# Taking the paddings out ahead of the feed-forward tiles of a Fourier mixer: the same program at other SBUF addresses

## The chip, the core and the metric

The kernel runs on one core of one Trainium2 chip. The metric is the device time of one execution in microseconds; the kernel before stands at 2060.12 us, the median of three runs (2059.15 to 2062.64).

## What is computed

The reference, cut to what matters (4 sequences of 3072 tokens, width 256):

```python
X = np.fft.rfft(x, axis=1)                      # Fourier mixing
Yr = Xr @ w_r - Xi @ w_i + b_r;  Yi = Xr @ w_i + Xi @ w_r + b_i
Y = soft_threshold(Yr, 0.01) + 1j * soft_threshold(Yi, 0.01)
x = np.fft.irfft(Y, n=3072, axis=1)
xk = mu_k * x + (1 - mu_k) * x_prev;  xr = mu_r * x + (1 - mu_r) * x_prev
k = np.maximum(xk @ w_k, 0)                     # first feed-forward, 256 -> 1024 -> 256
x = 1 / (1 + np.exp(-(xr @ w_rr))) * ((k * k) @ w_v)
h = x @ w_in                                    # second feed-forward, 256 -> 2048 -> 256
return (h * np.clip(h + 3, 0, 6) / 6) @ w_out
```

## The kernel before

Every matrix is held as two float32r parts, a rounded high part (`_hi`, `h`) and the rest (`_lo`, `l`), and a product is three matmuls: high by high, low by high, high by low. In a row of the trace a matmul reads `out<-moving,weights` or with the two inputs in the other order; the instruction's first operand in the code is the stationary one (the weights of the array, 128 columns, loaded by a LDWEIGHTS of its own), the second is the moving one.

Three kinds of work follow each other. The Fourier stages (`s1`, `s2`, `mix`, `ia`, `ib`) are woven with the first feed-forward: for each of 24 token tiles of 512 there is one unit `pr` (12 matmuls), four of `pk` (12 each) and four of `acc` (12 each), so 2592 matmuls with 512 moving columns. In `pr` and `pk` the weights `wr`, `wk` are stationary and the inputs `kh`, `kl` move; in `acc` the weights `wv` are stationary and the squared outputs `gh`, `gl` move. The second feed-forward's first tile (`pi`, 512 columns) runs in between. From the second tile on, each of 184 units (23 tiles by 8) has 45 matmuls of 256 moving columns: 21 of a Strassen-like product (into `rq` and `cc`), whose stationary operand is either a sum of weights (`sw`) or a part of the weights (`wi`) and whose moving operand is an input or a sum of inputs (`xh`, `xl`, `th`, `tl`); and 24 into `oacc`, where the gate outputs `gh`, `gl` are stationary and `wo` moves. The code lists all instructions of each engine in a fixed order.

Tiles of one pool lie one behind the other in each partition of SBUF, and nearly every size is a multiple of 256 bytes. So a small tile that is never used, made by `pad(pool, n)`, shifts all that the pool (and the pools opened behind it) allocates later by n bytes modulo 256. Such calls stand ahead of several groups of tiles.

Of the kernel before, what the change touches and what calls it, by code (L numbers as in the profile page):

```python
# [103 lines left out]
def fourier_mix_ffn_kernel(  # L104
# [33 lines left out]
    kb = ctx.enter_context(tc.tile_pool(name="kb", bufs=1))  # L138
    kw = ctx.enter_context(ExitStack())
    kw_p = kw.enter_context(tc.tile_pool(name="kw", bufs=1))  # L140
# [3 lines left out]
    def pad(pool, n):  # L144

        pads.append(n)
        pool.tile([128, n // 4], F32, name=f"pad{len(pads)}")
# [82 lines left out]
                running.append(w.decode(w.load(stage, *job), *job))  # L230
            yield

    padded = []

    def stage1():
        w = kb.tile([128, 1024], U32, tag="gh", bufs=3, name="stw")
        t = kb.tile([128, 2, TOK], F32, tag="gl", bufs=3, name="stt")
        if not padded:
            padded.append(pad(kb, 128))
        return w, t  # L240

    with tc.manual_schedule(engines=order):
# [249 lines left out]
            later.append(plan("ib", b, 0, 8))  # L492

        aw = [Weights(fp, w, 2, D, f"aw{i}") for i, w in enumerate((w_r, w_i))]
        pad(kw_p, 64)
        wr = Weights(kw_p, w_rr, 2, D, "wr")
        wk = Weights(kw_p, w_k, 2, FF1, "wk")
        pad(kw_p, 128)
        wv = Weights(kw_p, w_v, 8, D, "wv")

        nc.gpsimd.dma_start(out=f1.rearrange("p s n -> p (s n)"), in_=small[:, 0 : 2 * N1])
# [117 lines left out]
        def load_2(i):  # L619
            b, t = tiles[i]  # L620
            v = sc_x[b].rearrange("a p n -> p a n")[:, :, TOK * t : TOK * t + TOK]
            a = kb.tile([128, 2, TOK], F32, tag="xf", bufs=1, name="xa2")
            nc.sync.dma_start(out=a, in_=v)
            xt[i] = a
# [7 lines left out]
        def u_i(i, j, between=()):  # L632

            xh, xl = xt[i]
            p = ptile("pi")
            for m in range(2):
                c = slice(256 * j + 128 * m, 256 * j + 128 * m + 128)
                three(
                    p[:, 512 * m : 512 * m + 512],
                    [((wi.hi[:, k, c], wi.lo[:, k, c]), (xh[:, k], xl[:, k])) for k in range(2)],  # L640
                )
            g = kb.tile([128, 1024], F32, tag="g", bufs=2, name="g2")
            h = kb.tile([128, 1024], F32R, tag="gh", bufs=3, name="gh2")
            l = kb.tile([128, 1024], F32R, tag="gl", bufs=3, name="gl2")
            nc.scalar.activation(g, p, AF.Relu, bias=half, scale=1.0 / 6.0)
            nc.vector.scalar_tensor_tensor(g, g, 1.0, p, op0=ALU.min, op1=ALU.mult)
            nc.scalar.activation(h, g, AF.Copy)
            for f in between:
                f()
            nc.vector.tensor_sub(l, g, h.bitcast(F32))  # L650
            hg[i, j] = (h, l)
# [7 lines left out]
        def sums(sp, c):  # L659

            j = slice(2 * c, 2 * c + 2)
            h, l = (w[:, :, j] for w in sw)
            tmp = {}

            def full():
                a = tmp["a"] = kb.tile([128, 4, 2, 128], F32, tag="yt", bufs=1, name="wa")
                for k in range(2):
                    for m in range(2):
                        hi, lo = (
                            w[:, k, 512 * c : 512 * c + 512]  # L670
                            .rearrange("p (j m f) -> p j m f", j=2, m=2)[:, :, m]
                            .bitcast(F32)
                            for w in (wi.hi, wi.lo)
                        )
                        nc.vector.tensor_add(a[:, 2 * m + k], hi, lo)

            def four():
                a11, a12, a21, a22 = (tmp["a"][:, n] for n in range(4))
                t = tmp["t"] = sp.tile([128, 4, 2, 128], F32, tag="t", bufs=1, name="ws")
                nc.vector.tensor_add(t[:, 0], a21, a22)  # L680
                nc.vector.tensor_sub(t[:, 1], t[:, 0], a11)
                nc.vector.tensor_sub(t[:, 2], a11, a21)
                nc.vector.tensor_sub(t[:, 3], a12, t[:, 1])

            return [
                (full, None),
                (four, lambda: nc.scalar.activation(h, tmp["t"], AF.Copy)),
                (lambda: nc.vector.tensor_sub(l, tmp["t"], h.bitcast(F32)), None),
            ]
# [215 lines left out]
        def decode_to(n):  # L905

            nonlocal done2
            while done2 < n:
                next(jobs2, None)
                done2 += 1  # L910
# [74 lines left out]
        for n, (i, j) in enumerate(units):  # L985
            if i == 0:
                decode_to(max(done2 + 2, 2 * (j // 2 * 2 + 1) + 7, 2 * (8 + j) + 7))
                if j == 3:
                    decode_to(len(wi.jobs + wo.jobs) * 2 + 5)
                    stage.close()  # L990
                    sp = ctx.enter_context(tc.tile_pool(name="sp", bufs=1))
                    pad(sp, 64)
                    sw = [sp.tile([128, 4, 8, 128], F32R, name=f"sw{c}") for c in range(2)]
                    pad(sp, 192)
                    c0, c1, c2, c3 = (sums(sp, c) for c in range(4))
                    x1 = split_s(sp, 1)

                    beside = {
                        3: ([x1[0][0]], [x1[0][1]]),
                        4: ([x1[1][0]], [x1[1][1], c0[0][0]]),  # L1000
                        5: ([x1[2][0]], [c0[1][0]]),
                        6: ([c1[0][0]], [c0[1][1], c0[2][0]]),
                        7: ([c1[1][0]], [c1[1][1]]),
                    }
                    both = lambda f, g: lambda: (f(), g())
                    aside = [(both(c1[2][0], c2[0][0]), None), c2[1], (both(c2[2][0], c3[0][0]), None)] + c3[1:]
                u_i(i, j, beside[j][0] if j >= 3 else ())
                if lag:
                    u_v(*lag.pop(0))
                    if not lag:  # L1010
                        kw.close()
                elif j > 2:
                    for f in u_o(*pend.pop(0)):
                        f()
                if j >= 3:
                    for f in beside[j][1]:
                        f()
            else:
                if (i, j) == (1, 0):
                    banks.close()  # L1020
                    pz = ctx.enter_context(tc.tile_pool(name="pz", bufs=6, space=PSUM))
                before = u_s(sp, pz, i, j, u_o(*pend.pop(0)), before, aside.pop(0) if aside else (None, None))
            pend.append((i, j))
            if i + 1 < len(tiles):
                if j == (1 if i else 0):
                    load_2(i + 1)
                if j == 3 and i:
                    aside += split_s(sp, i + 1)
# [28 lines left out]
```

## Time and profile before

| | |
|---|---|
| median of three runs | 2060.12 us |
| the profiled execution: its time / its span | 2060.34 / 2058.6 us |
| TensorE matmul busy | 2000.5 us, 97% of the span, 13928 matmuls |
| TensorE weight load busy | 1848.1 us, 90% |
| VectorE / ScalarE busy | 1529.6 us (74%) / 1353.3 us (66%) |
| mean granted TensorE clock | 0.982 of full |

How to read it: a matmul's busy time in the records includes the emptying of the array, so neighbours overlap. What a matmul costs in a full queue is the distance from its start to the next one's start. In the steady stretches below, recorded length minus distance is 163 ns throughout (281 against 118, 276 against 113), so that a group's mean length shows its distance as well.

### The profile page before, as it was taken

How to read it: one execution, taken by the hardware profiler on the slowest of the kernel's cores; microseconds unless marked ns; L12 is line 12 of the kernel's file. 1: busy time of each engine (PE TensorE's matmuls, PEld its weight loads, DVE VectorE, ACT ScalarE, POOL GpSimd, SP SyncE). 2: the span in 40 equal slices, each digit the busy share in tenths (PEclk: the TensorE clock that was granted, in tenths of full speed). 3: DMA queues.
4: the chain of work that ended last, by engine and by line, in shares of the span. 5: the costliest groups of instructions: out<-in, count | busy, mean ns of one | idle time of the engine just before them, and what ended most of it. 6: DMA issues, size and time to landing. Idle time of an engine off the chain costs nothing.

```text
span 2058.6 us, 33814 instructions
## 1 busy us (share of the span) xinstructions
PE 2000.5 (97%) x13928; PEld 1848.1 (90%) x13928; DVE 1529.6 (74%) x1929; ACT 1353.3 (66%) x1965; POOL 34.6 (2%) x63
## 2 busy tenths in 40 slices
PE   5889999999999999999999999999999999999999
PEld 3868888888788888877789999999999999999998
DVE  3778667766776687887878777777777777777775
ACT  5567557655765566666557766677666776677675
POOL 0000000000000000000000000000000000000000
PEclk7978999999999999999999999999999999999999
DMA  9775337543653352222101010010100110010100
GB/s 259 232 220 184 116 115 230 166 143 112 222 171 113 94 159 90 76 86 76 52 21 31 23 32 22 22 32 22 32 22 25 29 32 21 22 32 22 32 11 22
DMA packets 106989, 175.86 MB, mean 85 GB/s; under 512 B 12945, under 2 KB 63314, under 8 KB 106834
## 3 DMA queue, kind: packets, MB, share of 16 engines
q1 hardware_dynamic: 96034, 141.76, 22.4%
q0 software_dynamic: 10480, 31.67, 5.6%
q8 instruction: 109, 1.79, 0.4%
q14 instruction: 46, 0.38, 0.1%
q10 hardware_dynamic: 320, 0.26, 0.0%
HBM read 110.35 MB, written 63.31 MB: 84 GB/s over the span
## 4 chain that ended last, share of the span: by engine, by line
PE 80%; DVE 10%; ACT 5%; DMA 3%; issue 1%; SPq 0%; ACTq 0%; DVEq 0%
PE oacc L824 25%; PE rq L824 15%; PE acc L163 9%; PE pk L163 8%; PE cc L824 6%; PE mix L163 5%; PE s L163 4%; PE pr L163 2%; DVE g L591 2%; DVE gl L592 1%; PE ia L163 1%; PE ib L454 1%; PE pi L163 1%; PE ib L455 1%; DVE xf L549 1%
## 5 line engine op out<-in xcount | busy, mean ns | idle before, releaser
L824 PE MATMUL oacc<-wo_hi,gl 128*128 128x256 f32 x1536 | 431.6, 281 | 0.5 <-DVE gl L798 0.5
L824 PE MATMUL oacc<-wo_hi,gh 128*128 128x256 f32 x1536 | 430.7, 280 | 0.0
L824 PE MATMUL oacc<-wo_lo,gh 128*128 128x256 f32 x1536 | 430.4, 280 | 0.0
L824 PEld LDWEIGHTS oacc<-wo_hi,gh 128*128 128x128 f32 x1536 | 293.1, 191 | 0.2
L824 PEld LDWEIGHTS oacc<-wo_hi,gl 128*128 128x128 f32 x1536 | 289.3, 188 | 0.9 <-DVE gl L798 0.7
L824 PEld LDWEIGHTS oacc<-wo_lo,gh 128*128 128x128 f32 x1536 | 288.4, 188 | 0.0
L780 DVE TENSOR_TENSOR c<-rq,s 128x512 f32<-128x512 f32 x184 | 127.3, 692 | 182.9 <-ACT s L776 182.9
L793 DVE SCALAR_TENSOR_TENSOR g<-g,c 128x1024 f32<-128x1024 f32 x184 | 225.4, 1225 | 40.3 <-ACT g L792 35.0
L797 ACT ACTIVATE gh<-g 128x1024 fp32r<-128x1024 f32 x184 | 194.8, 1059 | 48.7 <-DVE g L793 48.6
L798 DVE TENSOR_TENSOR gl<-g,gh 128x1024 fp32r<-128x1024 f32 x184 | 223.7, 1216 | 1.2 <-ACT gh L797 1.2
L824 PE MATMUL rq<-th,sw 128*128 128x256 f32 x1104 | 222.1, 284 | 0.8 <-ACT s L771 0.6
L792 ACT ACTIVATE g<-c,half 128x1024 f32<-128x1024 f32 x184 | 210.7, 1145 | 4.3 <-DVE c L781 3.5
L760 ACT ACTIVATE s<-rq 128x512 f32<-128x512 f32 x184 | 110.3, 599 | 125.0 <-PE rq L824 123.1
L591 DVE TENSOR_TENSOR g<-g 128x1024 f32<-128x1024 f32 x96 | 117.4, 1222 | 79.8 <-ACT gh L590 79.8
L824 PEld LDWEIGHTS rq<-th,sw 128*128 128x128 f32 x1104 | 168.7, 188 | 1.6 <-ACT s L771 1.0
L163 PE MATMUL acc<-gl,wv_hi 128*128 128x512 f32 x384 | 153.4, 399 | 4.4 <-DVE gl L592 4.3
L824 PE MATMUL rq<-tl,sw 128*128 128x256 f32 x552 | 154.9, 281 | 0.0
L163 PE MATMUL pk<-kh,wk_hi 128*128 128x512 f32 x384 | 152.5, 397 | 0.8 <-ACT g L586 0.8
L163 PE MATMUL acc<-gh,wv_hi 128*128 128x512 f32 x384 | 153.2, 399 | 0.0
L163 PE MATMUL acc<-gh,wv_lo 128*128 128x512 f32 x384 | 152.6, 397 | 0.0
L163 PE MATMUL pk<-kh,wk_lo 128*128 128x512 f32 x384 | 151.6, 395 | 0.0
L163 PE MATMUL pk<-kl,wk_hi 128*128 128x512 f32 x384 | 151.4, 394 | 0.0
(152 smaller groups left out, 4902.4 us busy)
## 6 DMA issues: line engine op xcount, KB each, us to landing
tt<-in_tab_dram POOLq DMA_DIRECT2D x40, 640.0 KB, 4.8
yt<-sc_y SPq DMA_DIRECT2D x23, 608.0 KB, 4.0
a<-in_x_dram SPq DMA_DIRECT2D x64, 192.0 KB, 3.8
sc_a<-s1sb SPq DMA_DIRECT2D x32, 384.0 KB, 3.7
a<-sc_a SPq DMA_DIRECT2D x48, 256.0 KB, 3.2
sc_b<-iasb SPq DMA_DIRECT2D x48, 256.0 KB, 4.3
a<-sc_b SPq DMA_DIRECT2D x64, 192.0 KB, 3.1
sc_y<-ysb SPq DMA_DIRECT2D x32, 384.0 KB, 2.8
```

What stands on the lines that cost most here:

```text
L163: nc.tensor.matmul(o, a, c, start=first and i == 0, stop=last and i == n - 1, **kw)
L454: nc.tensor.matmul(o, h[:, i, e], r, start=True, stop=False)
L455: nc.tensor.matmul(o, l[:, i, e], r, start=False, stop=True)
L549: nc.vector.scalar_tensor_tensor(o, y[:, a, 0 : hi - lo], mus[:, w, a : a + 1], o, op0=ALU.mult, op1=ALU.add)
L591: nc.vector.tensor_mul(g, g, g)
L760: nc.scalar.activation(s[:, 1:3].rearrange("p a n -> p (a n)"), rq, AF.Copy)
L780: nc.vector.tensor_add(c[:, 1::2], two(rq), s[:, 0:2])
L792: nc.scalar.activation(g, c, AF.Relu, bias=half, scale=1.0 / 6.0)
L793: nc.vector.scalar_tensor_tensor(g, g, 1.0, c, op0=ALU.min, op1=ALU.mult)
L797: lambda: nc.scalar.activation(h, g, AF.Copy),
L798: lambda: nc.vector.tensor_sub(l, g, h.bitcast(F32)),
L824: return lambda: nc.tensor.matmul(o, lhs, rhs, start=start, stop=stop, skip_group_check=True)
```

## The change

Five `pad` calls go: one in the pool `kb` behind the tiles `gh`, `gl`; two in `kw_p`, ahead of `wr` and ahead of `wv`; two in `sp`, ahead of the weight sums and ahead of the tiles behind them. No instruction, no order and no wait changes on any engine; line numbers behind the edits drop by 4 to 8. Only start addresses move:

| tiles | address modulo 256 before | after |
|---|---|---|
| `kh`, `kl`, `xh`, `xl`, `xf`, `g`, `r`, `yt` (pool `kb`) | 160 | 32 |
| `th`, `tl`, `s`, `c`, temporaries (pool `sp`) | 160 | 32 |
| `wr`, `wk` | 224 | 32 |
| `wv` | 96 | 32 |
| `sw` | 224 | 32 |
| `gh`, `gl` | 32 | 32 |
| `wi`, `wo` | 224 | 224 |
| all tiles of the Fourier stages | | unchanged |

```diff
-    padded = []
-
     def stage1():
         w = kb.tile([128, 1024], U32, tag="gh", bufs=3, name="stw")
         t = kb.tile([128, 2, TOK], F32, tag="gl", bufs=3, name="stt")
-        if not padded:
-            padded.append(pad(kb, 128))
         return w, t
...
         aw = [Weights(fp, w, 2, D, f"aw{i}") for i, w in enumerate((w_r, w_i))]
-        pad(kw_p, 64)
         wr = Weights(kw_p, w_rr, 2, D, "wr")
         wk = Weights(kw_p, w_k, 2, FF1, "wk")
-        pad(kw_p, 128)
         wv = Weights(kw_p, w_v, 8, D, "wv")
...
                     sp = ctx.enter_context(tc.tile_pool(name="sp", bufs=1))
-                    pad(sp, 64)
                     sw = [sp.tile([128, 4, 8, 128], F32R, name=f"sw{c}") for c in range(2)]
-                    pad(sp, 192)
                     c0, c1, c2, c3 = (sums(sp, c) for c in range(4))
```

The text below speaks of a **pair**: a matmul's moving operand and the stationary operand of the matmul behind it, whose load runs beside it. A pair's **distance apart** is the stationary address minus the moving address, modulo 256. All slices begin at multiples of 256 bytes within their tiles here, so the table above gives it. Pairs in a unit of the second feed-forward, and in the first feed-forward:

| pairs | before | after |
|---|---|---|
| 24 pairs that `oacc` streams, per unit | 21 at 64, 3 at 0 (ahead of `rq`) | 24 at 64 |
| 21 pairs that `rq` and `cc` stream, per unit | 18 at 64, 3 at 128 (ahead of `oacc`) | 12 at 0, 9 at 192 |
| 2592 that `pr`, `pk`, `acc` stream | 2401 at 64, the rest at hand-overs | 2536 at 0 |
| 96 that `pi` streams | 89 at 64 | 89 at 192 |

## Rows read from the trace of the kernel before

**Rows 1.** The page: span, and busy time of each engine with instruction counts.
```profile
span 2058.6 us, 33814 instructions
...
PE 2000.5 (97%) x13928; PEld 1848.1 (90%) x13928; DVE 1529.6 (74%) x1929; ACT 1353.3 (66%) x1965; POOL 34.6 (2%) x63
```

**Rows 2.** Busy time by stretch: length, each engine, then PEclk, DMA share, GB/s.
```profile
400.00:820.00 420.00, 417.88 (x2414) 361.96 (x2413) 293.31 (x370) 260.46 (x364) 13.26 (x23) 1.00 0.44 136
820.00:1060.00 240.00, 235.62 (x1044) 189.69 (x1043) 196.10 (x239) 145.18 (x174) 0.00 (x0) 1.00 0.21 68
1075.00:1600.00 525.00, 524.69 (x4453) 524.28 (x4452) 407.34 (x494) 370.44 (x559) 0.00 (x0) 1.00 0.10 26
```

**Rows 3.** Matmul groups, 1100 to 2040 us: busy us, mean ns; idle before.
```profile
L824 PE MATMUL oacc<-wo_hi,gl 128*128 128x256 f32 x1420 | 399.2, 281 | 0.0
...
L824 PE MATMUL rq<-th,sw 128*128 128x256 f32 x1066 | 214.1, 283 | 0.0
L824 PE MATMUL rq<-tl,sw 128*128 128x256 f32 x533 | 149.6, 281 | 0.0
L824 PE MATMUL rq<-xh,sw 128*128 128x256 f32 x354 | 69.0, 276 | 0.0
L824 PE MATMUL cc<-tl,wi_hi 128*128 128x256 f32 x177 | 50.1, 283 | 0.0
...
L824 PE MATMUL cc<-xh,wi_hi 128*128 128x256 f32 x177 | 49.7, 281 | 0.0
...
L824 PE MATMUL rq<-xl,sw 128*128 128x256 f32 x177 | 49.2, 278 | 0.0
```

**Rows 4.** Timeline of one unit, TensorE: start us, length us, engine, line, instruction.
```profile
1500.26 0.28 PE L824 MATMUL cc<-tl,wi_hi 128*128 128x256 f32 x1
...
1500.50 0.28 PE L824 MATMUL oacc<-wo_hi,gl 128*128 128x256 f32 x1
1500.50 0.19 PEld L824 LDWEIGHTS oacc<-wo_lo,gh 128*128 128x128 f32 x1
...
1505.56 0.28 PE L824 MATMUL cc<-tl,wi_hi 128*128 128x256 f32 x1
```

**Rows 5.** Timeline of the last unit's unbroken `oacc` run, TensorE.
```profile
2046.11 0.28 PE L824 MATMUL oacc<-wo_lo,gh 128*128 128x256 f32 x1
...
2050.19 0.28 PE L824 MATMUL oacc<-wo_lo,gh 128*128 128x256 f32 x1
```

**Rows 6.** Timeline from the end of `acc` over a `mix` run, TensorE.
```profile
646.36 0.40 PE L163 MATMUL acc<-gl,wv_hi 128*128 128x512 f32 x1
646.60 0.28 PE L163 MATMUL mix<-aw_hi,Xh 128*128 128x256 f32 x1
...
647.18 0.28 PE L163 MATMUL mix<-aw_lo,Xh 128*128 128x256 f32 x1
...
649.34 0.39 PE L163 MATMUL pr<-kh,wr_hi 128*128 128x512 f32 x1
```

**Rows 7.** The matmul right behind a hand-over 0 apart, at 1501.4 us.
```profile
L824 PE MATMUL rq<-th,sw 128*128 128x256 f32 x1 | 0.3, 286 | 0.0
```

**Rows 8.** Timeline of the first feed-forward, from one `acc` unit to another, TensorE.
```profile
777.09 0.39 PE L163 MATMUL acc<-gh,wv_hi 128*128 128x512 f32 x1
777.32 0.39 PE L163 MATMUL acc<-gh,wv_lo 128*128 128x512 f32 x1
777.54 0.40 PE L163 MATMUL acc<-gl,wv_hi 128*128 128x512 f32 x1
...
791.05 0.39 PE L163 MATMUL acc<-gh,wv_hi 128*128 128x512 f32 x1
```

**Rows 9.** Timeline of a Fourier stage with 192 moving columns, TensorE.
```profile
642.55 0.27 PE L163 MATMUL s<-tt,al 128*128 128x192 f32 x1
...
643.78 0.42 PE L163 MATMUL acc<-gh,wv_hi 128*128 128x512 f32 x1
```

**Rows 10.** VectorE groups, 1100 to 2040 us: busy us, mean ns; idle before.
```profile
L798 DVE TENSOR_TENSOR gl<-g,gh 128x1024 fp32r<-128x1024 f32 x177 | 215.1, 1215 | 0.0
...
L722 DVE TENSOR_TENSOR tl<-xs,th 128x1024 fp32r<-128x1024 f32 x22 | 26.8, 1218 | 0.0
```

## The prediction

> **What bounds the kernel now.** The page's busy line first: TensorE is busy for 97% of the span, VectorE for 74%, ScalarE for 66% [rows 1]. A share over the whole says little, so next the stretches. From 400 to 820 us, where the Fourier stages and the first feed-forward are woven, TensorE is busy for 417.9 of 420 us; from 820 to 1060 us, mostly feed-forward, for 235.6 of 240; in the second feed-forward for 524.7 of 525, with the granted clock at 1.00 (the 2.4 GHz level) in all three, while VectorE has 407.3 of 525 [rows 2]. There the matmul groups show no idle time before them [rows 3]. So neither a wait nor a transfer ends last: the queue of TensorE does, and what counts is the distance from one matmul's start to the next. A nanosecond on each matmul of the second feed-forward's products is 3864 x 1 ns = 3.9 us on the kernel; the end after the last matmul does not change.
>
> What that distance is, the timeline shows. One unit of 45 matmuls takes 1505.56 - 1500.26 = 5.30 us, 117.8 ns each [rows 4]. The 36 matmuls of the last unbroken `oacc` stretch take 4.08 us, 113.3 ns each [rows 5], with the same tiles, shape and granted clock, and a `mix` stretch has 19 in 2.16 us, 113.7 ns [rows 6]. So there are at least two levels for one shape. Group means show where each stands in the unit: lengths of 276 ns go with 113, 281 with 118, 283 with 120 [rows 3]. No engine's wait explains the difference, since nothing waits. A matmul and the load for the next one start together: the rows at 1500.50 are such a pair [rows 4]. That is the only place at which an address can matter to TensorE, and both stretches at the short distance, [rows 5] and the later part of [rows 6], consist of pairs 64 apart alone.
>
> **The change part by part.** No instruction, wait or transfer is added or removed. Three things could still have a price.
>
> *The operands of VectorE, ScalarE and the DMAs.* They move by 128 bytes or stay. The subtraction that reads at 160 and 32 and writes at 32 takes 1215 ns, the one that reads and writes at 160 alone 1218 ns [rows 10]. I take 0; the cover is 117.7 us of VectorE's idle time in those 525 [rows 2], so that even 3 ns on each operation would not show.
>
> *The 21 products per unit of `rq` and `cc`.* Their pairs go from 64 (18) and 128 (3) apart to 0 (12) and 192 (9). Today their lengths sum to 6 x 283 + 3 x 281 + 2 x 276 + 278 + 283 + 8 x 281 = 5902 ns (the last eight are the groups with `wi` stationary, of which one stands as a row), less 21 x 163 = 2479 ns [rows 3]. What a lasting run of pairs 0 apart costs, no row shows. The nearest is the hand-over from `oacc` to `rq`, 0 apart now, three times a unit: the matmul right behind it reads 286 ns in one case [rows 7], and the group of the first two of each trio averages 283 [rows 3], against 281 of the ones around. I take 120 ns for all 21: 2520 - 2479 = +41 ns a unit, x 184 = **+7.5 us**. Lower bound: all 21 at the 113.3 of the unbroken `oacc` stretch, 2379 ns, -100 ns a unit, -18.4 us. Upper bound: all at the 286 level, 123 ns, 2583 ns, +104 ns a unit, +19.1 us. I take the middle one because it is the mean over all such hand-overs and the upper one is a single case. For 192 apart there is no row at 256 columns; I give it the same price.
>
> *The 2536 pairs of the first feed-forward that go from 64 to 0 apart.* From one `acc` unit to another, 60 matmuls take 13.96 us, 232.7 ns each, or 116.3 per 256 columns [rows 8]. The load beside them is shorter: in the stage with 192 columns, where the moving operand is too short to be the limit, a matmul takes 1.23 us / 11 = 112 ns [rows 9]. So only about half of a 512-column stream has a load beside it. That half goes to 120: +3.7 ns, x 2536 = **+9.3 us**. The bounds: both halves at 113.3 is 6.1 ns less, -15.5 us; both at 123 is 13.3 ns more, +33.7 us. One sign against a price is the pair (0 apart) from `acc` to `mix`: 646.36 to 646.60 us, 0.24 us, no more than the 0.23 of the others [rows 6, 8]; but in the second feed-forward too it is the matmul behind the pair that is long. The 89 pairs of `pi` are 89 x 3.7 ns = 0.3 us.
>
> *The 24 matmuls of `oacc`.* Three of their pairs improve from 0 to 64 apart, the others stay; they run at 118 now, broken up by hand-overs three times a unit, and will be. I take 0. Were they to fall to the 113.3 of the unbroken run, it is -24 x 4.5 ns x 184 = -19.9 us.
>
> Sum: 7.5 + 9.3 + 0.3 = +17.1 us on the profiled execution's 2060.3 us (span 2058.6 and 1.7 around it), which is 0.2 us from the median of the runs: **2077 us**.
>
> **The rivals.** *Addresses don't matter: 2060 us.* Then the two levels come from the order of the matmuls, whatever the tiles' places. For it: `oacc` pairs of equal distance take 113.3 in one place and 118 in another [rows 3, 5], and `rq<-xh,sw` has 276 ns in the middle of a unit. Against: the long matmuls of the unit stand right behind pairs that are not 64 apart ([rows 3, 7]; `cc<-tl`, which is 128 apart from the load beside it, has 283). The Trainium skill has a rule that speaks for this rival: "SBUF — State Buffer", section "Who interferes with whom", gives TensorE two read ports, one for the moving operand and one for the weights, and says that TensorE waits on nobody. By it the change does nothing and the sum is 0. This trace neither proves nor refutes it, but the spread from 276 to 286 ns at one shape and one granted clock is something that it leaves open.
>
> *64 apart is no better than others, and the products get faster: 2026 us.* The moving read and the load meet at 64 apart too, and it is the mixture of distances that keeps the unit at 118. After the change a `rq` run begins behind pairs at 64 and then stays at one or two distances. For it: `acc` matmuls behind the 192-apart hand-over are the shortest of their kind, 777.09 to 777.54 us for two, 225 ns each against 232.7 [rows 8], and all steady pairs 64 apart with 512 columns are above the 226.6 that two halves at 113.3 would take. If `rq`, `cc` and the first feed-forward all fall to 113.3 per 256 columns it is -18.4 - 15.5 = -34 us. It decides where the mean length of `rq<-th,sw` falls to 276 or below.
>
> *The clash is lasting and severe: 2113 us.* A pair 0 apart starts load and stream in the same place, and each delays the other again in the next pair, so that the 286 of the first matmul behind a hand-over stays: +19.1 + 33.7 = +53 us. If only loads are delayed, the first feed-forward is spared (232.7 ns against a load's 112) and the second pays, because 118 leaves 6 ns over the load. Against it: of the three matmuls of a trio only the first reads 286, the third averages 281.
>
> **How the numbers follow.** A measurement of this kernel can tell about 0.2% (4 us) from no change. Chances: slower in the mild way 0.45 (2066 to 2095), slower in the severe way 0.17 (2095 to 2130), no effect 0.14, faster 0.24 (mostly 2026 to 2055). The time is that of the likeliest, 2077. The range leaves out half of the faster case's depth and the severe case's top: 2044 to 2113. The sum of the cases gives 0.24 faster, 0.14 within 0.2%, 0.62 slower.
>
> **What would show it.** In the profile after, the order and the waits are the same and TensorE is still without idle time. If the step on the products is right, the groups `rq<-th,sw`, `rq<-xh,sw` and those of `wi` read about 283 ns instead of 276 to 283, a unit takes 5.34 us instead of 5.30, and `oacc` stays at 281. If the step on the first feed-forward is right, 60 matmuls of 512 columns take 14.18 us instead of 13.96. `mix`, `s2` and `ib`, whose tiles stay, keep their lengths; if they change, something else is at work. The prediction is wrong if `oacc` changes though its tiles stay, if 0 and 192 apart behave in opposite ways (192 is priced by nothing but the 0 apart beside it), or if the first feed-forward answers to the whole stream and not to half of it.

## The result: 2039.5 us, faster by 1.0%, and the profile after

The changed kernel takes **2039.52 us** (median of four runs, 2038.93 to 2039.9), the kernel before 2059.89 us (four runs): a ratio of 0.990, 95% interval 0.9888 to 0.9911. The prediction, 2077 us and slower, had the wrong sign, and the result lies below its range.

The page of the changed kernel, span and busy times, beside [rows 1]:

```profile
span 2038.1 us, 33814 instructions
...
PE 1976.6 (97%) x13928; PEld 1835.8 (90%) x13928; DVE 1528.7 (75%) x1929; ACT 1354.2 (66%) x1965; POOL 34.6 (2%) x63
```

The same instructions, and still a TensorE that is busy for 97%. The windows of [rows 2] (length, each engine's busy time and count, then granted clock, DMA share, GB/s):

```profile
820.00:1060.00 240.00, 232.94 (x1062) 190.61 (x1061) 196.61 (x243) 145.38 (x171) 0.00 (x0) 1.00 0.21 66
1075.00:1600.00 525.00, 524.56 (x4519) 524.17 (x4519) 415.20 (x503) 376.98 (x569) 0.00 (x0) 1.00 0.10 27
```

The clock is at the same level. In the second feed-forward the engine is as full as before, but 4519 matmuls fit into the 525 us where 4453 did. So each one costs less; no wait went away. Which ones, the groups from 1100 to 2040 us show (busy us, mean ns; idle before), beside [rows 3]:

```profile
L818 PE MATMUL oacc<-wo_hi,gh 128*128 128x256 f32 x1441 | 400.5, 278 | 0.0
...
L818 PE MATMUL oacc<-wo_lo,gh 128*128 128x256 f32 x1442 | 399.2, 277 | 0.0
L818 PE MATMUL rq<-th,sw 128*128 128x256 f32 x1062 | 208.8, 277 | 0.0
L818 PE MATMUL rq<-tl,sw 128*128 128x256 f32 x531 | 147.9, 278 | 0.0
L818 PE MATMUL rq<-xh,sw 128*128 128x256 f32 x354 | 70.9, 282 | 0.0
L818 PE MATMUL rq<-xl,sw 128*128 128x256 f32 x177 | 50.0, 283 | 0.0
L818 PE MATMUL cc<-xh,wi_hi 128*128 128x256 f32 x177 | 49.6, 280 | 0.0
```

`oacc`, whose tiles did not move, falls from 281 to 278 and 277. `rq<-th,sw` falls from 283 to 277, and `rq<-xh,sw` rises from 276 to 282. The timeline of one unit (start us, length us, engine, line, instruction), beside [rows 4], shows how `oacc` does it:

```profile
1500.05 0.28 PE L818 MATMUL rq<-xl,sw 128*128 128x256 f32 x1
...
1503.76 0.28 PE L818 MATMUL oacc<-wo_hi,gh 128*128 128x256 f32 x1
1503.89 0.28 PE L818 MATMUL oacc<-wo_hi,gl 128*128 128x256 f32 x1
1504.00 0.28 PE L818 MATMUL oacc<-wo_lo,gh 128*128 128x256 f32 x1
1504.12 0.28 PE L818 MATMUL oacc<-wo_hi,gh 128*128 128x256 f32 x1
...
1504.68 0.39 PE L818 MATMUL rq<-th,sw 128*128 128x256 f32 x2
...
1505.27 0.28 PE L818 MATMUL rq<-xl,sw 128*128 128x256 f32 x1
```

A unit takes 5.22 us where it took 5.30. The first `oacc` matmul behind the hand-over lasts 0.13 us to the next start, then the run speeds up: the five from 1504.12 to 1504.68 take 112 ns each, 113 by the median of all units. All three runs of a unit do so now. Before, two of the three stayed at 118 to their end, but the third, the one shown here from the kernel before, already fell to 113 for its last three matmuls (0.34 us here):

```profile
1503.92 0.28 PE L824 MATMUL oacc<-wo_hi,gh 128*128 128x256 f32 x1
...
1504.26 0.40 PE L824 MATMUL rq<-th,sw 128*128 128x256 f32 x2
```

That is so in 181 of 182 units (118, 120, 119, 123, 118, 113, 113, 113 ns by the median), and the group's mean of 281 in [rows 3] hides it. Next the first feed-forward, beside [rows 8], and a `mix` run, beside [rows 6]:

```profile
756.90 0.39 PE L163 MATMUL acc<-gh,wv_hi 128*128 128x512 f32 x1
...
767.78 0.39 PE L163 MATMUL acc<-gh,wv_hi 128*128 128x512 f32 x1
```

```profile
643.12 0.28 PE L163 MATMUL mix<-aw_hi,Xh 128*128 128x256 f32 x1
...
645.95 0.39 PE L163 MATMUL pr<-kh,wr_hi 128*128 128x512 f32 x1
```

48 matmuls of 512 columns take 10.88 us, 226.7 ns each (before 232.7). The 24 of `mix`, whose tiles did not move either, take 2.83 us, 117.9 ns each (before 2.74 us, 114.2 ns). Summed over one profiled execution of each kernel, from each matmul's start to the next one's (waits counted apart):

| us | before | after | difference |
|---|---|---|---|
| `pr`, `pk`, `acc` | 603.3 | 590.6 | -12.7 |
| `mix` | 132.1 | 134.8 | +2.7 |
| waits of TensorE ahead of the second feed-forward's units | 86.6 | 89.8 | +3.2 |
| start of those units (us from the span's start) | 1070.7 | 1064.5 | -6.2 |
| `oacc` in the units | 524.1 | 512.6 | -11.5 |
| `rq` and `cc` in the units | 456.2 | 453.2 | -3.0 |
| all units | 983.0 | 968.75 | -14.3 |

### The profile page after: what moved, and what is told of

It reads as the page before. It is cut to its first block, busy times and chain, and to the rows that moved or that the text cites. A ratio compares the mean times of both kernels' runs of the same rounds, so it can differ in the third digit from the quotient of the medians.

```text
span 2038.1 us, 33814 instructions
## 1 busy us (share of the span) xinstructions
PE 1976.6 (97%) x13928; PEld 1835.8 (90%) x13928; DVE 1528.7 (75%) x1929; ACT 1354.2 (66%) x1965; POOL 34.6 (2%) x63
## 4 chain that ended last, share of the span: by engine, by line
PE 80%; DVE 10%; ACT 5%; DMA 3%; issue 2%; SPq 0%; ACTq 0%; DVEq 0%
PE oacc L818 25%; PE rq L818 16%; PE acc L163 9%; PE pk L163 8%; PE cc L818 6%; PE mix L163 6%; PE s L163 4%; PE pr L163 2%; DVE g L585 2%; DVE gl L586 1%; PE ia L163 1%; PE pi L163 1%; PE ib L451 1%; PE ib L450 1%; DVE xf L543 1%
## 5 line engine op out<-in xcount | busy, mean ns | idle before, releaser
L818 PE MATMUL oacc<-wo_hi,gl 128*128 128x256 f32 x1536 | 426.7, 278 | 0.6 <-DVE gl L792 0.6
L818 PE MATMUL oacc<-wo_lo,gh 128*128 128x256 f32 x1536 | 425.4, 277 | 0.0
L818 PEld LDWEIGHTS oacc<-wo_hi,gh 128*128 128x128 f32 x1536 | 288.3, 188 | 0.2
L792 DVE TENSOR_TENSOR gl<-g,gh 128x1024 fp32r<-128x1024 f32 x184 | 223.5, 1215 | 1.2 <-ACT gh L791 1.2
L818 PE MATMUL rq<-th,sw 128*128 128x256 f32 x1104 | 217.5, 277 | 1.0 <-ACT s L765 0.7
```

The costliest lines, as they stand in the source:

```text
L792: lambda: nc.vector.tensor_sub(l, g, h.bitcast(F32)),
L818: return lambda: nc.tensor.matmul(o, lhs, rhs, start=start, stop=stop, skip_group_check=True)
```

## The experiments

All kernels below compute the reference in full; they differ in paddings, or where it is said in ScalarE's order and in repeated copies. The diffs leave out the empty list `padded` that some of them set up. "Rhythm" is the distance from one matmul's start to the next in a run; medians of it are worked out from all starts of the trace. The recorded length is the rhythm plus 163 ns here too, so that 276, 281 and 283 ns in a row are 113, 118 and 120.

### One part of the change at a time

**ff1_zero**: the kernel before, with one line less: `pk` comes to 0 apart at address 160, `acc` to 0 apart at 32.

```diff
-        pad(kw_p, 64)
         wr = Weights(kw_p, w_rr, 2, D, "wr")
```

> First feed-forward alone at 0 apart: kh, kl, wr, wk all at 160, gh, gl, wv at 32; the second feed-forward stands exactly as in the kernel before. Theory D (the distance apart within a lasting run decides, wherever the tiles lie): pr, pk and acc take 226.7 ns a matmul instead of 233 although pk lies at 160 and not at 32, that is -6.1 ns x 2592 = -16 us; some of it is lost again in mix, which takes 118 instead of 113 behind them in the kernel after; the second feed-forward's unit stays at 5.30 us. About 2050. Rival A (operands at the place 32 are what helps): only acc, whose operands lie at 32, falls to 226.7, pk stays at 233; about 2053, told apart by pk. Rival H (only cleaner hand-overs help): no change in the middle of a run of pk, 2060.

2056.87 us, ratio 0.9979 (0.997 to 0.9988). `pk` and `acc` run at 227 and the second feed-forward is as before, unit 5300 ns. `mix` goes to 118, about 80 ns a run lost on average. So 0 apart is a better distance than 64 for 512 columns, at either address.

**ff2_zero**: the kernel before without the paddings of `sp`; `rq`'s pairs with `sw` at 0 apart, those with `wi` at 64.

```diff
-                    pad(sp, 64)
                     sw = [sp.tile([128, 4, 8, 128], F32R, name=f"sw{c}") for c in range(2)]
-                    pad(sp, 192)
```

> Second feed-forward's products alone: sw, th, xh all at 160 (0 apart), wi against them 64 apart as before; the first feed-forward stands exactly as in the kernel before. Hand-overs: oacc to rq 192 apart, rq to oacc 128 apart. Theory D: the trio of rq with th takes 348 ns as in the kernel after instead of 359, and oacc gets closer to 113; the unit falls from 5.30 to 5.20 to 5.25 us, so -9 to -18 us, 2042 to 2051. Rival A (place 32): nothing lies at 32 but gh, so 5.30 and 2060. Rival H (the hand-over back to oacc at 0 apart instead of 128 is what brought oacc to 113): with that hand-over at 128 still, oacc stays at 281 ns in length, the unit at 5.28 to 5.30, 2056 to 2060.

2055.97 us, ratio 0.9976 (0.9966 to 0.9985), unit 5280 ns. Its timeline has both kinds of `oacc` run in one unit:

```profile
1500.66 0.28 PE L824 MATMUL oacc<-wo_hi,gh 128*128 128x256 f32 x1
...
1501.60 0.40 PE L824 MATMUL rq<-th,sw 128*128 128x256 f32 x2
...
1502.32 0.28 PE L824 MATMUL oacc<-wo_lo,gh 128*128 128x256 f32 x1
1502.43 0.28 PE L824 MATMUL oacc<-wo_hi,gh 128*128 128x256 f32 x1
1502.56 0.28 PE L824 MATMUL oacc<-wo_hi,gl 128*128 128x256 f32 x1
1502.67 0.28 PE L824 MATMUL oacc<-wo_lo,gh 128*128 128x256 f32 x1
...
1503.24 0.40 PE L824 MATMUL rq<-th,sw 128*128 128x256 f32 x2
```

The eight behind `cc` (which runs at 118) take 0.94 us, 117.5 ns each, to the end. The eight behind `rq` (which runs at 120) take 0.92 us, and the last five of them 0.57, 114 each. Both hand-overs are 128 apart and both runs 64 apart. What a run came from decides its rhythm, beside its own distance.

**ff2_after**: the changed kernel, with the first feed-forward put back to 64 apart.

```diff
+        pad(kw_p, 64)
         wr = Weights(kw_p, w_rr, 2, D, "wr")
```

> The complement of the run on the first feed-forward alone: the second feed-forward exactly as in the kernel after (products 0 and 192 apart, all hand-overs as there), the first feed-forward at 64 apart as before (kh 32, wk and wv 96, gh 32). Theory R (each run of one distance locks into one of a few start-to-start distances: 113.3, 117.7 or 120 ns per 256 columns; which one depends on the distance apart and on the hand-over ahead of it): the unit at 5.22 us as in after, pk and acc at 233, mix back at 113: about 2060 - 14.7 = 2045. Rival A (place 32 itself): pk, whose operands lie at 32 and 96, below 233. Rival (the parts interact across the two feed-forwards): the unit back at 5.30, 2060.

2045.96 us, ratio 0.9927 (0.9912 to 0.9942). The unit is 5220 ns and the 512-column matmuls are at 233. `mix` is split: of its 35 unbroken runs after 200 us, 18 fall to 113 and 17 stay at 118. One of each kind (shortest, median and longest ns, first and last start):

```profile
L163 PE MATMUL mix<-aw_hi,Xh x8: 276/276/279, 291.0 to 293.4; 128*128 128x256 f32 x8
```

```profile
L163 PE MATMUL mix<-aw_hi,Xh x8: 281/281/282, 301.4 to 303.9; 128*128 128x256 f32 x8
```

The starts of the trace tell which run does what. 32 of the 35 begin behind a 512-column matmul, at a hand-over 0 apart. The 17 in which that matmul took 235 to 237 ns to the start of `mix` fall; the 15 in which it took 228 to 230 stay. So at equal distances it matters where in the turn of 236 and 231 the hand-over comes. The kernel before has the same hand-over from `acc` into `mix`: 12 runs fall behind 235 or 236, two stay behind 229. In the changed kernel all 32 are left at 225 to 227, and all stay at 118.

### The size of the effect at other distances

**ff1_128_192**: the changed kernel, with `pk` 128 apart and `acc` 192 apart.

```diff
+        pad(kw_p, 128)
         wr = Weights(kw_p, w_rr, 2, D, "wr")
...
+        pad(kw_p, 64)
         wv = Weights(kw_p, w_v, 8, D, "wv")
```

> The kernel after with two paddings in the first feed-forward: kh at 32 and wk, wr at 160 (128 apart), gh at 32 and wv at 224 (192 apart); the second feed-forward as in the kernel after. Theory D with 0 as the only good distance: pk and acc both lose the 226.7 of the kernel after and take about 233, 14 to 17 us more than after, 2054 to 2057. Rival (64 is the one bad distance, all others are good): both stay at 226.7, 2040. Rival (the distance counts by how late the moving read meets the load: 0 good, then 192, 128, 64): pk at 230 to 233 and acc at 227 to 230, 2045 to 2052.

2044.13 us, ratio 0.9922 (0.9907 to 0.9937). `pk` takes 233 on the mean (a quarter of its runs 229 and 237 in turn, most of the others 228 to 233 with a single 240), `acc` 229 (226, 229 and 232 in turn); `mix` is at 113 in 31 of 35 runs, as in the kernel before.

**prod_zero**: all pairs within the products of a unit at 0 apart, and the first feed-forward too; `oacc` and the hand-overs into it at 64. Against the kernel before:

```diff
-            padded.append(pad(kb, 128))
+            padded.append(pad(kb, 192))
...
-        pad(kw_p, 64)
         wr = Weights(kw_p, w_rr, 2, D, "wr")
...
-        pad(kw_p, 128)
+        pad(kw_p, 64)
...
-                    pad(sp, 64)
...
-                    pad(sp, 192)
```

> All products of the second feed-forward at 0 apart, wi as well: xh, th, sw, wi all at 224; first feed-forward also at 0 apart (pk at 224, acc at 32); oacc 64 apart as ever, hand-overs oacc to rq 0 apart, rq to oacc 64 apart. Theory D: the nine matmuls with wi fall from 117.6 to about 113, 9 x 4.3 x 184 = -7 us against the kernel after, and rq with th to 113 throughout, another -5: about 2028. Rival A (place 32): products at 224 lose what the kernel after gained, 2050 to 2060. Rival H (hand-overs): oacc to rq 0 apart as in the kernel before disturbs each run, the unit goes back to 5.27 to 5.30, 2050 to 2056.

2065.82 us, ratio 1.0026 (1.0017 to 1.0035): slower, in spite of the first feed-forward's 227. Its groups:

```profile
L823 PE MATMUL oacc<-wo_hi,gh 128*128 128x256 f32 x1409 | 395.9, 281 | 0.0
...
L823 PE MATMUL rq<-th,sw 128*128 128x256 f32 x1058 | 213.2, 283 | 0.0
...
L823 PE MATMUL cc<-th,wi_lo 128*128 128x256 f32 x176 | 49.8, 283 | 0.0
```

The products run at 120, the price that the prediction gave them. `oacc` stays at 118, and the unit is 5340 ns, the very 5.34 that was predicted for the changed kernel.

**ff_zero**: every pair of both feed-forwards at 0 apart, at address 224.

```diff
     def stage1():
+        if not padded:
+            padded.append(pad(kb, 192))
         w = kb.tile([128, 1024], U32, tag="gh", bufs=3, name="stw")
```

> Every pair of both feed-forwards at 0 apart, oacc and all hand-overs too (kh, gh, wr, wk, wv, sw, th, xh at 224 with wi and wo). Theory R with 120 as the rhythm of a lasting run of 256 columns at 0 apart, as the products showed with all of them at 0: unit 45 x 120 = 5.40 us, +18 us in the second feed-forward, -3 to -6 in the first: 2072 to 2075. Rival (it is the mixture of 0 with 64 that gave 120 there): products at 113 to 118, unit 5.10 to 5.30, 2020 to 2057.

2076.34 us, ratio 1.0071 (1.0056 to 1.0086). Groups from 1100 to 2040 us, and two rows of the timeline of the first feed-forward:

```profile
L822 PE MATMUL oacc<-wo_lo,gh 128*128 128x256 f32 x1392 | 394.3, 283 | 0.0
...
L822 PE MATMUL rq<-th,sw 128*128 128x256 f32 x1044 | 210.5, 283 | 0.0
...
L822 PE MATMUL cc<-th,wi_lo 128*128 128x256 f32 x174 | 49.3, 283 | 0.0
```

```profile
766.48 0.39 PE L163 MATMUL acc<-gl,wv_hi 128*128 128x512 f32 x1
...
777.36 0.39 PE L163 MATMUL acc<-gl,wv_hi 128*128 128x512 f32 x1
```

Every 256-column matmul is at 120 and a unit takes 5400 ns, while 48 matmuls of 512 columns take 10.88 us, 226.7 ns each. Of the distances tried, one is the worst for one length of stream and the best for the other.

**all_zero**: the same with the Fourier stages at 0 apart too. Against the changed kernel (the first padding also moves the pools opened behind it):

```diff
-        pad(cst, 32)
+        pad(cst, 96)
...
-        pad(cst, 128)
...
-        pad_a, pad_t, pad_y = [128], [192], [192]
+        pad_a, pad_t, pad_y = [], [], []
```

> Every tile of the whole program at 224, so that the Fourier stages too have their pairs at 0 apart. Theory R with 120 for lasting runs of 256 columns at 0: mix and ia go to 120 as well (132 us of mix to 138), the second feed-forward to 5.40 a unit: 2078 to 2084. Rival (120 belongs to the second feed-forward's way of going through its tiles): mix at 113 to 118, 2070 to 2076.

2076.8 us, ratio 1.007 (1.0054 to 1.0085). The rows of `mix` (shortest, median and longest ns), first of the kernel before, then of all_zero:

```profile
L163 PE MATMUL mix<-aw_hi,Xh x384: 276/276/468, 51.8 to 707.1; 128*128 128x256 f32 x192
```

```profile
L163 PE MATMUL mix<-aw_hi,Xh x384: 277/283/487, 52.5 to 708.0; 128*128 128x256 f32 x192
```

The rule is not one of the second feed-forward: `mix` goes to 120 as well.

### Addresses or distances, and the hand-overs

**mod64_0**: the changed kernel with every tile moved down by 32 bytes, all distances kept.

```diff
-        pad(cst, 32)
...
-        pad_a, pad_t, pad_y = [128], [192], [192]
+        pad_a, pad_t, pad_y, pad_e = [128], [192], [192], [32]
...
+                if pad_e:
+                    pad(fp, pad_e.pop())
...
+                    pad(w2, 32)
```

> The kernel after with every tile of the whole program moved down by 32 bytes, so that all distances apart stay and all addresses become multiples of 64. Theory that only distances count: every length as in after, 2039 to 2040. Rival L (the reads go in blocks of 64 bytes, and a slice that begins in the middle of one needs one block more: 33 instead of 32 for 512 columns, 17 instead of 16 for 256): 512 columns 226.7 x 32/33 = 220 ns, 256 columns 113.3 x 16/17 = 107 at best, -17 us in the first feed-forward and up to -40 in the second: 1985 to 2020. Rival (the places are worse at multiples of 64): slower than after.

2041.11 us, ratio 0.9902 (0.9885 to 0.9918). The unit is 5220 ns, and the groups read as those of the changed kernel to within 1 ns. So the distance counts and the place, over these 32 bytes, does not:

```profile
L821 PE MATMUL oacc<-wo_lo,gh 128*128 128x256 f32 x1445 | 400.2, 277 | 0.0
L821 PE MATMUL rq<-th,sw 128*128 128x256 f32 x1064 | 209.3, 277 | 0.0
```

**after_wi64**: the changed kernel with `wi` moved by 128 bytes, its pairs 64 apart; hand-overs into `oacc` at 0 apart as in the changed kernel.

```diff
                     wi = Weights(w2, w_in, 2, FF2, "wi")
+                    pad(w2, 128)
                     wo = Weights(w2, w_out, 16, D, "wo")
```

> The kernel after with the nine matmuls against wi at 64 apart instead of 192 (wi at 96; xh, th, sw at 32); hand-overs as in after (0 into oacc, 64 out). Theory R with 113.3 open to pairs 64 apart: the nine fall from 117.5 towards 113.3 where the matmuls ahead leave them a disturbed rhythm, unit 5.18 to 5.22, 2032 to 2040. Rival: they lock at 117.7, as the nine did before, and oacc is reached from another rhythm: unit 5.22 to 5.27, 2040 to 2049.

2044.06 us, ratio 0.9923 (0.9906 to 0.9939), unit 5233 ns. The matmuls on `wi` fall to 113, but the unit grows:

```profile
L820 PE MATMUL oacc<-wo_hi,gl 128*128 128x256 f32 x1443 | 403.4, 280 | 0.6 <-DVE gl L794 0.6
...
L820 PE MATMUL cc<-xh,wi_lo 128*128 128x256 f32 x177 | 48.9, 276 | 0.0
```

By place in the unit, the `oacc` run behind `cc` now stays at 118; the two behind `rq` still fall to 113, one of them late. Behind the same hand-over, at the same place in the unit, a run that comes from 118 falls to 113 (the changed kernel) and one that comes from 113 goes to 118 (here).

**shift128, prod64_e0, prod64_e192**: three more settings of the hand-overs. shift128 keeps the products' 0 and 192 apart with hand-overs of 128 in and 192 out; the other two have all products at 64 apart and hand-overs of 0 in and 128 out, or 192 both ways. Against the changed kernel (the first padding of shift128 and of prod64_e192 stands behind `gh` and `gl`, as in the kernel before):

```diff
# shift128
+            padded.append(pad(kb, 128))
+        pad(kw_p, 128)                    # ahead of wv
+                    pad(w2, 128)          # ahead of wo
# prod64_e0
+                    pad(w2, 128)
+                    pad(sp, 64)           # ahead of sw
+                    pad(sp, 192)          # behind sw
# prod64_e192
+            padded.append(pad(kb, 64))
+        pad(kw_p, 192)
+                    pad(w2, 64)
+                    pad(sp, 64)
+                    pad(sp, 192)
```

> The kernel after with all operands of the products moved by 128 (xh, th, sw at 160, wi at 96): distances within the products as in after (0 and 192), but the hand-overs are now 128 apart into oacc (0 in after) and 192 apart out of it (64 in after). First feed-forward still at 0 apart. Theory H2 (the distance at the hand-over into oacc sets the rhythm of the eight that follow): oacc back at 281 ns in length, unit 5.28 to 5.30, 2050 to 2056. Rival P (the rhythm in which the products leave off decides, and that comes from their own distances): oacc stays at 277 to 278, unit 5.22, 2040.

> Products 64 apart throughout as before (xh, th at 32, sw and wi at 96), hand-over into oacc 0 apart as in after, out of it 128 apart; first feed-forward at 0 apart. Theory H2: oacc at 277 to 278 ns in length as in after, products between 276 and 281: unit 5.15 to 5.22, 2028 to 2040. Rival P: oacc as in the kernel before, 281, unit 5.30, 2055.

> Products 64 apart throughout (xh, th at 96, sw and wi at 160), both hand-overs 192 apart; first feed-forward at 0 apart (pk at 96, acc at 32). Theory H2 without a rule for 192: oacc at 276 if 192 throws it out of 117.7 as 0 does, else 281; unit 5.15 or 5.30, 2028 or 2055. Rival P: 5.30, 2055. Beside the run with 0 into oacc it tells whether any break of distance serves or 0 alone.

| kernel | us, ratio (interval) | unit | an `oacc` run (each 64 apart) |
|---|---|---|---|
| shift128 | 2044.98, 0.9924 (0.9909 to 0.9939) | 5233 | behind `rq` (117 to 121) falls to 113; behind `cc` (113) goes to 118 |
| prod64_e0 | 2046.03, 0.993 (0.9915 to 0.9945) | 5253 | behind products at 118: 121, 122, 116, 114, 113 ... |
| prod64_e192 | 2054.22, 0.9972 (0.9961 to 0.9984) | 5273 | behind products at 118: 118, 117, 117, 119, 116, 114, 113, 113 |

In prod64_e0 the products are at 64 apart as before the change and `oacc` falls all the same: its gain comes with the hand-over and does not need the products' new distance. 192 apart does it too, but two matmuls later.

**ff_shift64**: the changed kernel with both feed-forwards moved up by 64 bytes, so that only the hand-overs to and from the Fourier stages change.

```diff
+            padded.append(pad(kb, 64))
...
                     wo = Weights(w2, w_out, 16, D, "wo")
+                    pad(w2, 192)
```

> After, with every tile of both feed-forwards moved up by 64 bytes: within the feed-forwards all distances stay as in after, only the hand-overs between them and the Fourier stages change (into mix from 0 to 192 apart, out of mix from 64 to 128). Theory 1 (the hand-over into mix at 0 apart is what puts mix at 117.7): mix returns to 113.3 and the sum falls by about 3 us, to 2036 to 2038 us, with the unit at 5.22 us and 512-column matmuls at 227. Theory 2 (whatever comes from matmuls at 226.7 starts mix at 117.7): all lengths as in after and 2039.5 us. Rival: an absolute place plays a part, then the unit or the 227 changes as well.

2042.27 us, ratio 0.9914 (0.99 to 0.9927); units and 512-column matmuls as in the changed kernel, and `mix` not moved:

```profile
L163 PE MATMUL mix<-aw_hi,Xh x384: 276/281/468, 52.6 to 705.6; 128*128 128x256 f32 x192
```

The first theory falls: with 192 apart in place of 0 at the hand-over, `mix` is as slow.

### Can the unit be held at 113?

**ff2_all64**: every pair of the second feed-forward, hand-overs included, at 64 apart; the first feed-forward at 0. Against the kernel before:

```diff
-            padded.append(pad(kb, 128))
+            padded.append(pad(kb, 192))
...
-        pad(kw_p, 64)
...
-        pad(kw_p, 128)
+        pad(kw_p, 64)
...
                     wi = Weights(w2, w_in, 2, FF2, "wi")
+                    pad(w2, 192)
                     wo = Weights(w2, w_out, 16, D, "wo")
```

> First feed-forward at 0 apart; in the second every pair at 64 apart, hand-overs too (moving xh, th, wo at 224, stationary sw, wi, gh at 32; wi and wo are parted by a padding of their own). Theory R with hand-overs at another distance as what throws a run out of 113: with none left, rq, cc and oacc stay at 113.3 as the last oacc stretch of the kernel before does: unit 45 x 113.3 = 5.10 us, -37 us against before in this half, about -3 in the other: 2020. Rival (117.7 is a rhythm as lasting as 113.3 at 64 apart, and nothing in the unit kicks it out): unit 5.30, about 2056.

2057.17 us, ratio 0.9978 (0.9965 to 0.9991), and a spread of 2050.82 to 2060.42 over ten executions, where the changed kernel's four lie within 1 us. The spread by itself shows nothing: the kernel before, executed beside it, has 2057.91 to 2064.38. The trace does. The groups of one execution, first from 1100 to 1290 us, then from 1320 to 2040 us:

```profile
L823 PE MATMUL oacc<-wo_hi,gh 128*128 128x256 f32 x297 | 82.1, 276 | 0.0
...
L823 PE MATMUL rq<-xh,sw 128*128 128x256 f32 x74 | 14.4, 276 | 0.0
```

```profile
L823 PE MATMUL oacc<-wo_hi,gh 128*128 128x256 f32 x1094 | 307.6, 281 | 0.0
...
L823 PE MATMUL rq<-xh,sw 128*128 128x256 f32 x270 | 53.9, 281 | 0.0
```

One program, the same addresses, and two rhythms: units of 5100 ns (45 x 113.3) up to 1300 us, then 5300 to the end. The turn comes behind a matmul that starts some 20 ns late, with the one behind it another 0.1 us late. Four such pairs between 1215 and 1270 us had left 5100 as it was.

Whether such a wait turns it, four kernels ask. **all64_defer** moves ScalarE's work for the next tile behind the next unit's gate, to take the small waits away; **after_defer** does the same to the changed kernel as a control. **all64_waits** is all64_defer with four deliberate waits (a copy made five times in four units); **all64_redraw** is ff2_all64 with a short one in every tile.

```diff
# all64_defer, after_defer
             if before:
                 before[0]()
+            if late:
+                late.pop()()
...
             if on_scalar:
-                on_scalar()
+                late.append(on_scalar)
# all64_waits, besides
+            for _ in range(5 if (i, j) in ((6, 2), (11, 2), (16, 2), (20, 2)) else 1):
                 nc.scalar.activation(s[:, 1:3].rearrange("p a n -> p (a n)"), rq, AF.Copy)
# all64_redraw
             nc.scalar.activation(s[:, 1:3].rearrange("p a n -> p (a n)"), rq, AF.Copy)
+            if j == 2:
+                nc.scalar.activation(s[:, 1:3].rearrange("p a n -> p (a n)"), rq, AF.Copy)
+                nc.scalar.activation(s[:, 2], q, AF.Copy)
```

> The second feed-forward with every pair at 64 apart, as tried, and ScalarE's work on the next tile (which made the copy of rq late every eighth unit, so that TensorE waited 20 to 40 ns there) put behind the gate of the following unit. Theory W (at 64 apart both 113.3 and 117.7 keep themselves up; only a wait of TensorE draws anew): with the waits gone after the first tile, most of the 184 units stay at one value, 5.10 us where the last early wait drew 113.3 (it did so in 8 of 10 waits looked at): 2020 to 2030, or 2055 where it drew 117.7. Rival F (the short distance gives way by itself after some 40 units): units go to 5.30 without a wait before it, 2048 to 2057.

> The kernel after with the same move of ScalarE's work, as a control. Theory W: the kernel after sets its rhythm anew at each hand-over in every unit and had no waits there, so nothing changes: 2039 to 2040, unit 5.22. Rival (the move itself saves time): below 2036.

> The first of these with a copy repeated four more times in four single units (tiles 6, 11, 16 and 20), so that TensorE waits about 1 us there. Theory W: the length of a unit changes between 5.10 and 5.30 behind some of the four and nowhere else; time 2025 to 2060 by what is drawn. Rival F: changes elsewhere too, without a wait.

> The second feed-forward with every pair at 64 apart, and in one unit of every tile the copy of rq done once more, and half of it a third time, so that TensorE waits some 0.1 to 0.6 us there. Theory W: the rhythm is drawn anew in every tile instead of once, and 113.3 comes in about 4 of 5 draws, as behind the short waits seen so far: mean unit 5.14 us, waits 23 x 0.5 = 11 us, second feed-forward 957 us against 969 in the kernel after: 2027 to 2040. Rival (waits draw 117.7 as often as not): 2040 to 2055.

| kernel | us, ratio (interval) | lowest to highest | units in the profiled execution |
|---|---|---|---|
| all64_defer | 2053.59, 0.9965 (0.9952 to 0.9977) | 2050.1 to 2058.7 | 5300 from the 8th to the end, no wait in them; the 7th turns behind a start 12 ns late |
| after_defer | 2043.5, 0.9915 (0.9902 to 0.9927) | 2041.0 to 2045.5 | 145 of 182 at 5220; one or two of 5253 to 5287 in each tile |
| all64_waits | 2057.23, 0.9975 (0.9963 to 0.9986) | 2049.0 to 2060.8 | 5100 and 5300, changes only behind a wait |
| all64_redraw | 2054.61, 0.997 (0.9959 to 0.998) | 2051.8 to 2058.3 | about half at 5100, half at 5300 |

The timeline of all64_waits around its second deliberate wait shows a turn (in brackets the idle time before a matmul and what ended it):

```profile
1484.56 0.40 PE L828 MATMUL rq<-xh,sw 128*128 128x256 f32 x2
...
1489.86 0.40 PE L828 MATMUL rq<-xh,sw 128*128 128x256 f32 x2
...
1496.58 0.50 PE L828 MATMUL rq<-th,sw 128*128 128x256 f32 x2 [1.62 <-ACT s L762]
...
1497.04 0.40 PE L828 MATMUL rq<-xh,sw 128*128 128x256 f32 x2
...
1502.15 0.39 PE L828 MATMUL rq<-xh,sw 128*128 128x256 f32 x2
1507.25 0.39 PE L828 MATMUL rq<-xh,sw 128*128 128x256 f32 x2
```

The unit from 1484.56 takes 5.30 us. Behind the wait, the one from 1497.04 takes 5.11 and the next 5.10. Of the four deliberate waits two turned 5300 into 5100, one 5100 into 5300, and one left 5300. In all64_redraw, of 22 long waits (units of 5569 to 5712 ns) 15 were followed by 5100 and seven by 5300. No rhythm changed without a late start ahead of it, and neither rhythm was held through all of them. The outcome is no toss, though. In all64_redraw it goes by the length of the wait to a nanosecond or two: out of 5300, the seven waits that left 424 or 425 ns between two starts ended in 5300 and the eight with 425 to 427 in 5100; out of 5100, all seven with 485 stayed. Setting a wait that finely was not tried. A kernel with all units at 5100 would end 0.12 x 184 = 22 us before the changed one; none of these did. None of the 18 kernels beats the changed one.

## Why the prediction was wrong

**What bounds the kernel** was right: TensorE's queue, start to start, and only the operands' addresses. The first rival (addresses don't matter) is out: the changed kernel and ff_zero have the same instructions in the same order and are 37 us apart (35 by their ratios). The rule of the Trainium skill that spoke for it ("SBUF — State Buffer", section "Who interferes with whom": two read ports, TensorE waits on nobody) does not cover this; the measurement decides.

**The step with the wrong mechanism is `oacc`'s: "they run at 118 now, broken up by hand-overs three times a unit, and will be. I take 0."** They gave 11.5 of the 20.5 us, more than half of the listed bound of -19.9. The premise behind it was that a pair's cost belongs to its own distance. The runs show that at 64 apart two rhythms each keep themselves going (ff2_all64, one program), and that the hand-over into the run and the rhythm that it comes from pick one. Before, `cc` and `rq` at 118 handed over at 128 apart and two of a unit's three `oacc` runs stayed at 118; now they hand over at 0 apart and all three fall to 113. That the products' own distance isn't needed for it, prod64_e0 shows. "They run at 118 now" was also a mean taken for a level: the third run already ended at 113. The prediction did name the sign of it ("wrong if `oacc` changes though its tiles stay") and had [rows 5] against [rows 3], equal distance at two rhythms, in hand.

**The step on the first feed-forward: "That half goes to 120: +3.7 ns, x 2536 = +9.3 us."** This is the largest miss, 22 us. Measured -12.7 us in the matmuls: 226.7 ns instead of 233. The price of 256 columns was carried to 512, and ff_zero shows the two going opposite ways at 0 apart. The bound "both halves at 113.3" (-15.5 us) was the right end; the shortest matmuls of [rows 8] pointed there. Of the 12.7, `mix` gave back 2.7 and longer waits of TensorE 3.2.

**The products: "I take 120 ns for all 21", +7.5 us.** The price of a lasting run was right, as prod_zero and ff_zero show, but there was no lasting run: the matmuls on `sw` stand in runs of three and six behind hand-overs, where the rhythm still goes from 112 to 121 ns, and the nine at 192 apart take 118, not 120. Measured -3.0 us. Pricing 192 like 0 was the named weak spot.

**The second rival** (faster, 2026 us) had the sign and its reason, "64 apart is no better than others", and was right on the first feed-forward (-15.5 us in its sum, -12.7 measured). It put the rest, -18.4 us, on the products, which gave 3.0, and had nothing for `oacc`; that `rq<-th,sw` nearly met its sign (276 asked, 277 read) is luck, since the products as a whole fell by 3.0 us alone. **The third** (lasting and severe) has its mechanism in ff_zero, at 120 and not at 123. The reading set against it, that only the first of a trio is long, does not hold: before the change the second took 119 to 122 ns by the median.

**What stays open.** What in the engine makes the rhythms, and why a few nanoseconds at a hand-over or a wait decide between them. For `mix`, the hand-over's own length sorts the runs without exception where it is 0 apart (ff2_after), and behind a first feed-forward at 226.7 every run stays at 118; but this is a sorting of rows, and no edit set that length alone. Nor does any run tell whether a moving operand meets the next matmul's weights or its own: within a run both give the same distance.

## What to carry to other kernels

Where TensorE is full and runs one shape, read the distance between starts, not busy shares: if one shape has more than one rhythm at the same granted clock, a per cent or two may lie in the operands' start addresses (2039.5 to 2076.8 us here). Price each length of stream and each lasting distance by a run of its own, and don't carry a price from 256 columns to 512 or from a hand-over to a lasting run. Measure a padding in the whole kernel: a stage whose tiles stay can change by what runs ahead of it, so gains need not add up. The two halves of this change do (0.9979 and 0.9927 alone, 0.990 together); within the second feed-forward, after_wi64 makes nine matmuls faster and the unit longer.

## What the runs showed of the hardware that was not expected

- Lasting rhythms by distance apart (stationary minus moving address, modulo 256), in stretches with a granted clock of 0.99 to 1.00:

| apart | 512 columns | 256 columns |
|---|---|---|
| 0 | 226.7 ns (ff1_zero, after, ff_zero) | 120 (prod_zero, ff_zero, all_zero) |
| 64 | 233.3, mostly as 236 and 231 in turn (before) | 113.3 or 117.7 (ff2_all64) |
| 128 | 233, in part as 229 and 237 in turn (ff1_128_192) | not tried as a lasting run |
| 192 | 229 (ff1_128_192) | 113 (shift128) or 118 (after) |

- The times come in steps. At the 2.4 GHz level 113.3, 120, 226.7 and 233.3 ns are 272, 288, 544 and 560 clocks, all multiples of 16. The other rhythms come out so over a whole cycle (three of 117.7 are 353 ns, three of 229 are 687, 236 and 231 together 467), and every median unit measured (5100, 5220, 5233, 5253, 5273, 5280, 5300, 5340 and 5400 ns) is within 0.4 ns of a multiple of 16 clocks (6.67 ns). That is arithmetic on the rows; what steps by 16 no run shows.
- A stream of full matmuls can hold either of two rhythms at the same addresses for 170 units and more (all64_defer), and every change of rhythm seen inside such a stream stands behind a late start, of 12 ns in the smallest case: 4% of a stage, and the 12 ns stand in no list of waits.
